# First batch's value loads, masks and weight split rebuilt, seven-product sums kept in PSUM, and a new order of work, in a banded attention and gated MLP kernel

## The chip, the cores and the metric

The kernel runs on one core of one Trainium2 chip. The metric is the device time of one execution in microseconds; three runs of the kernel before are given, and the median counts.

## What is computed

Eight batches, eight heads, 576 positions, head size 64. Four heads ("near") see the last 32 positions, four ("far") see every fourth of the last 128. The attention output is laid out as 576 x 512 per batch and goes through a gated MLP with a spatial product. Cut to what matters:

```python
scores = scale * np.matmul(q, k.transpose(0, 1, 3, 2))
scores = np.where(masks[None], scores, -1e9)          # near heads: mask_plain, far heads: mask_dil
attn = np.exp(scores - scores.max(-1, keepdims=True))
attn = attn / (attn.sum(-1, keepdims=True) + 1e-09)
x = (attn @ v).transpose(0, 2, 1, 3).reshape(B, S, H * D)
h = np.maximum(x @ w_in, 0.0)                          # 512 -> 1024
u, v = h[..., :512], h[..., 512:]
v_n = (v - mean(v)) / np.sqrt(var(v) + 1e-06)
v_s = np.einsum('ts,bsd->btd', w_spatial, v_n) + b_spatial[None, :, None]
out = (u * v_s) @ w_out                                # 512 -> 512
```

`w_in` and `w_out` arrive as 64-bit floats, all else as 32-bit floats.

## The kernel before

Every product that needs full precision is made of three passes over a high and a low part (`PASSES`, L276). The far heads' positions are reordered on the host, so that both kinds of head become a band: 18 blocks of 32 queries against 64 keys each.

**Planner.** The class `Timeline` (L26 to L142) runs at build time. Each piece of work is a generator ("strand") that asks for buffers by tag, waits for keys that other strands have set, and names an engine and a cost per step. The planner takes the strand whose start plus a small weight times its rank is lowest, and so fixes the order on every engine (L1094). Ranks come from the formulas and the tables `shift`, `second` and `first` (L930 to L1028). The tables hold no work, only order. All loads go through SP's queue, in the order of the list `first` (L916). Eight PSUM banks (`bank`) are shared; `mm` (4), `s`, `pt` and `av` limit how many of a kind are open.

**Start.** `warm` (L889) issues 512-column products of zeros whenever TensorE has nothing better, as long as the planner's time is under 30 us. The masks are made on GpSimd and copied into place on VectorE (L229 to L253). `weight` (L300) splits each 512-column half of `w_in` and each quarter of `w_out`, 12 pieces in all, from a 64-bit float into two parts: a scaled copy on ScalarE (L319), a shift with the sign masked out (L321), a merge of the sign (L323), a mask (L326) and a product (L329) on VectorE. The low part is then finished by TensorE (L335 to L339), VectorE or GpSimd. `spatial` (L365) splits the spatial weight; for two of its four large pieces TensorE makes the difference (L381, L382), for the others VectorE does.

**Attention of one batch.** `heads_in` and `values_in` load a head pair. `values_in` (L443) uses four DMAs per pair, each of 64 partitions with pieces of 64 values (256 bytes). `unit` (L455) does a sixth of a batch: products of 64x32 tiles (L469), scaling with the mask added (L489), the row maximum (L491), then for `u < 2` six exponentials with the running sum (L497) and for `u == 2` a subtraction on GpSimd (L504), one exponential (L506) and the sum on VectorE (L508). The result is scaled (L512) and transposed (L517). `weighted` (L526) multiplies by the values (L545) in two halves per group of two head pairs, and `evacuated` (L566) copies each into `raw` (L572).

**MLP of one batch.** `features_in` (L576) splits `raw` into two parts; `v_tile` (L599) makes the second half of `h` and normalises it; `upper` (L681) makes the first half in batch 0; `gate` (L699) makes the spatial product and multiplies (L718). The product with `w_out`, and from batch 1 on the one for `u`, use a seven-product scheme on 2 x 2 blocks. `factor` (L775) splits the factors, `differences` (L812) makes them on GpSimd, `product` (L824, matmul L831) makes one product, and `piece` (L846) adds it in: product 11 is copied by ScalarE (L874), every other product is added to a running tile by VectorE (L872). Per half `m` that is one copy and seven adds; finished tiles go to `out` through SP (L883). There are 15 such sums (8 for `o`, 7 for `u`), each with two halves.

Of the kernel before, what the change touches and what calls it, by code (L numbers as in the profile page):

```python
# [22 lines left out]
NEG = -(2.0**100)  # L23

# [123 lines left out]
def tile_banded_attention_gated_moe(  # L148
# [22 lines left out]
    nc = tc.nc  # L171
# [29 lines left out]
    def bufs(tag, shape, n, pool=const):  # L201
# [6 lines left out]
            mm=[None] * 4,  # L208
            s=[None] * 2,
# [20 lines left out]
    kinds = tl.bufs["raw"][0][:, : 2 * KW].bitcast(BF16).rearrange("p (n k) -> p n k", n=4)  # L230
# [20 lines left out]
    for (far, g), n in cut.items():  # L251
        r = slice(g % 2 * 2 * QB, g % 2 * 2 * QB + 2 * QB)
        nc.vector.tensor_copy(masks[r, US * far + g // 2], kinds[r, n])  # L253
# [4 lines left out]
    nc.vector.tensor_scalar_mul(minus, draft, -1.0)  # L258
    ident = plus.bitcast(F32)
    halfneg = const.tile([P, 1], F32, name="halfneg")  # L260
    nc.gpsimd.memset(halfneg, -0.5)

# [13 lines left out]
    PASSES = ((0, 0), (0, 1), (1, 0))  # L276
    PE, ACT, DVE, DVE2, POOL, DMA = "PE", "ACT", "DVE", "DVE2", "POOL", "DMA"
# [8 lines left out]

    staged = {}

    def weight_in(key, src):

        yield "kqv"
        (staged[key],) = yield DMA, 1.95, 1.5
        dtype = src[0].dtype
        place = staged[key][1][:, : 512 if dtype == F32 else 1024]
        rows = P // len(src)
        for i, part in enumerate(src):
            nc.sync.dma_start(place[i * rows : i * rows + rows].bitcast(dtype), part)
        tl.done("in", *key)

    def weight(key, hi, lo, dtype, how):  # L300
# [23 lines left out]
        tl.add(-0.15 + key[-1] * 0.01, rounded(hi, g, ("hi", *key)))  # L324
# [34 lines left out]
    def spatial_in(sc):  # L359
        yield "kqv"  # L360
        (staged[sc],) = yield DMA, 1.1, 1.5
        nc.sync.dma_start(staged[sc][1][:, :S], w_spT[:, sc, :])
        tl.done("in", sc)

    def spatial(sc):  # L365
# [6 lines left out]
        if sc < 4:  # L372
            nc.scalar.copy(wt[0][:, sc, :], w)
            if not (sc in (1, 2,)):
                yield DVE2, 0.75
                sub(wt[1][:, sc, :], w, wt[0][:, sc, :])
            for ts in (slice(0, HS), slice(HS, S)) if sc in (1, 2,) else ():
# [45 lines left out]
    def heads_in(b, hp, lo=0, hi=NU):  # L423
# [5 lines left out]
        got = yield DMA, 0.74 * (hi - lo), 1.5  # L429
# [13 lines left out]
    def values_in(b, hp):  # L443

        yield "kqv"
        (big,) = yield DMA, 3.3, 1.5
        src = vw[b, hp].rearrange("k (t j d) -> k t j d", j=2, d=D)
        dst = big[1][:, :BIG].rearrange("p (t n d) -> p t n d", n=2, d=D)
        for j in range(2):
            for n in range(2):  # L450
                nc.sync.dma_start(dst[j * D : j * D + D, :, n, :], src[n * QB : n * QB + KW, :, j, :])
# [3 lines left out]
    def unit(b, G, u):  # L455
# [3 lines left out]
        yield [("qk", b, hp, u) for hp in pairs] + ([("v", 0, 1)] if b == 1 else [])  # L459
        yield "s bank bank p"  # L460
        *held, pb = yield PE, 0.52, 0.0
        s = [h[:, : US * KW].rearrange("p (e k) -> p e k", e=US) for _, h in held[1:]]
        for e in range(US):
            for q in range(4):
                g = 2 * (US * u + e) + q // 2
                kq = keys[b, pairs[q % 2]]
                for j in range(2):
                    r = slice(j * D, j * D + D)
                    nc.tensor.matmul(  # L469
                        s[j][q * QB : q * QB + QB, e, :],  # L470
                        kq[r, WIN + S :].rearrange("p (u n i t) -> p u t n i", n=2, i=QB, t=US)[:, u, g // 2 % US, g % 2],
                        kq[r, g * QB : g * QB + KW],
                        start=True,
                        stop=True,
                    )
# [7 lines left out]
        if G >= NG // 2:  # L483
            m = masks[:, US + US * u : 2 * US + US * u]
        else:
            m = masks[:, :US] if u == 0 else masks[:, 1:2].broadcast_to([P, US, KW])
        yield DVE, 1.08, 0.08
        for j in range(2):
            nc.vector.scalar_tensor_tensor(p[:, :, j, :], s[j], SCALE, m, op0=ALU.mult, op1=ALU.add)  # L489
        tl.give(*held)  # L490
        nc.vector.tensor_reduce(nm, flat, axis=AX.X, op=ALU.max, negate=True)  # L491
        if u < 2:
            for e in range(US):
                yield ACT, 0.664 + 0.115 * (e == US - 1), 0.1 * (e == US - 1)
                for j in range(2):
                    i = 2 * e + j
                    nc.scalar.activation(  # L497
                        p[:, e, j], p[:, e, j], AF.Exp, bias=nm[:, i : i + 1], accum_out=sm[:, i : i + 1]
                    )
            nc.scalar.activation(sm, sm, AF.Copy, bias=1e-9)  # L500
            yield DVE, 0.11, 0.085
        else:
            yield POOL, 0.79, 0.04
            nc.gpsimd.tensor_add(flat, flat, nm.unsqueeze(2).broadcast_to([P, 2 * US, KW]))  # L504
            yield ACT, 0.425, 0.1
            nc.scalar.activation(p, p, AF.Exp)  # L506
# [53 lines left out]

    raws = {}

# [118 lines left out]
    def upper(b, h, f):  # L681
        fs = slice(f * P, (f + 1) * P)
        ts = slice(h * HS, h * HS + HS)
        yield [("v", b, t) for t in range(4)] + [("wi", 0, c) for c in range(NC)]
# [475 lines left out]
```

## Time and profile before

| | |
|---|---|
| runs, us | 547.47, 547.51, 550.34 (median 547.51) |
| span of the profiled execution, us | 544.7 |
| around the span (median less span), us | 2.8 |
| PE busy | 536.1 us, 98% |
| DVE / ACT / POOL busy | 80% / 56% / 39% |
| TensorE clock, mean over the span | 1.000 |
| instructions | 18357 |
| moved by DMA | 56.65 MB, of 97446 packets 78290 under 512 B |

The span runs from the first to the last instruction of the core. The profiled execution's own time is not listed apart; its span and the 2.8 us around it make 547.5 us. PE is TensorE, DVE is VectorE, ACT is ScalarE, POOL is GpSimd, SP is the engine that issues the DMAs. A busy time of PE includes the pipelined ends of its products, so it says that something is under way, not that the array is at its peak.

### The profile page before, as it was taken

Reading aid. Unit: us, or ns where it says so; the run is one execution under the profiler, and the core shown is the slowest. Engines: PE = TensorE matmul, PEld = TensorE weight load, DVE = VectorE, ACT = ScalarE, POOL = GpSimd, SP = SyncE. Lnnn points to the kernel's source line nnn. Section 1 sums busy time; section 2 is a strip of 40 time slices with the busy share of each in tenths; the row PEclk is TensorE's granted clock in tenths of the full one; section 3 lists DMA queues with packets and bytes.
Section 4 is the critical chain, followed back from the end, with each engine's and each line's share of the span. In section 5 each row is a group of like instructions: output and inputs, shape, how many; then the busy total and the mean of one; then the engine's idle time right before and its main releaser. Section 6 shows DMA issues by size and latency. Waiting matters only on the chain.

```text
span 544.7 us, 18357 instructions
## 1 busy us (share of the span) xinstructions
PE 536.1 (98%) x7591; PEld 487.9 (90%) x7591; DVE 435.7 (80%) x1036; ACT 307.1 (56%) x939; POOL 215.1 (39%) x255
## 2 busy tenths in 40 slices
PE   9998999999999999999999999999999999999997
PEld 7766789999998899988999999988999899989997
DVE  5988778989956998489957998489956899479836
ACT  4787796455755555565454555556464565454312
POOL 3420385373426153524417163433417153253230
PEclk9999999999999999999999999999999999999999
DMA  8999741201463144511464135421454134301002
GB/s 236 250 185 339 162 105 59 91 22 66 109 160 91 45 134 90 150 52 55 113 127 132 45 113 106 122 75 56 113 121 147 44 113 94 65 12 44 34 1 87
DMA packets 97446, 56.65 MB, mean 104 GB/s; under 512 B 78290, under 2 KB 87506, under 8 KB 97364
## 3 DMA queue, kind: packets, MB, share of 16 engines
q1 hardware_dynamic: 97364, 55.50, 38.4%
q8 instruction: 59, 0.97, 0.8%
q14 instruction: 23, 0.19, 0.1%
HBM read 46.04 MB, written 9.44 MB: 102 GB/s over the span
## 4 chain that ended last, share of the span: by engine, by line
PE 93%; DMA 3%; ACT 2%; issue 1%; SPq 1%; DVE 0%; POOL 0%
PE bank L831 31%; PE bank L711 19%; PE bank L614 16%; PE bank L545 6%; PE bank L469 5%; PE bank L517 3%; PE bank L628 2%; PE bank L690 2%; PE bank L895 2%; PE bank L713 2%; PE bank L712 2%; PE bank L335 1%; DMA kqv<-in_vw_dram 1%; DMA kqv<-in_w_in_dram 1%; ACT p L497 1%
## 5 line engine op out<-in xcount | busy, mean ns | idle before, releaser
L872 DVE TENSOR_TENSOR ur<-ur,bank 128x288 f32<-128x288 f32 x210 | 87.4, 446 | 28.3 <-PE bank L831 27.9
L794 ACT CAST fac<-ur 128x288 fp32r<-128x288 f32 x112 | 46.0, 430 | 79.8 <-DVE ur L718 40.3
L711 PE MATMUL bank<-wth,vnh 128*128 128x288 f32 x256 | 76.5, 299 | 0.0
L280 DVE TENSOR_TENSOR fac<-ur,fac 128x288 fp32r<-128x288 f32 x112 | 60.5, 550 | 19.5 <-ACT fac L794 19.2
L711 PE MATMUL bank<-wth,vnl 128*128 128x288 f32 x256 | 75.6, 295 | 0.1
L711 PE MATMUL bank<-wtl,vnh 128*128 128x288 f32 x256 | 75.6, 295 | 0.0
L821 POOL TENSOR_TENSOR ur<-ur,ur 128x288 f32<-128x288 f32 x64 | 55.5, 877 | 44.1 <-DVE ur L718 34.0
L512 POOL TENSOR_TENSOR p<-p,rv 128x384 f32<-128x384 f32 x48 | 40.8, 851 | 74.5 <-DVE rv L510 63.4
L497 ACT ACTIVATE p<-p,nm 128x64 f32<-128x64 f32 x192 | 64.5, 337 | 8.8 <-DVE nm L491 8.7
L650 POOL TENSOR_TENSOR rs<-rs,halfneg 128x1 f32<-128x1 f32 (+1 forms) x40 | 29.3, 732 | 91.1 <-DVE rs L648 91.0
L831 PE MATMUL bank<-fac,woh 128*128 128x288 f32 x256 | 53.3, 298 | 0.1
L614 PE MATMUL bank<-wih,xl 128*128 128x512 f32 x128 | 50.1, 392 | 1.8 <-issue 1.8
L821 POOL TENSOR_TENSOR raw<-raw,raw 128x288 f32<-128x288 f32 x42 | 43.3, 1037 | 19.4 <-DVE fac L280 18.6
L614 PE MATMUL bank<-wih,xh 128*128 128x512 f32 x128 | 50.4, 394 | 0.0
L614 PE MATMUL bank<-wil,xh 128*128 128x512 f32 x128 | 50.2, 392 | 0.0
L711 PEld LDWEIGHTS bank<-wth,vnh 128*128 128x128 f32 x256 | 48.2, 188 | 0.4
L711 PEld LDWEIGHTS bank<-wth,vnl 128*128 128x128 f32 x256 | 48.1, 188 | 0.3 <-issue 0.3
L711 PEld LDWEIGHTS bank<-wtl,vnh 128*128 128x128 f32 x256 | 48.2, 188 | 0.0
L831 PEld LDWEIGHTS bank<-fac,woh 128*128 128x128 f32 x256 | 42.2, 189 | 2.4 <-ACT raw L572 0.4
L831 PE MATMUL bank<-fac,o 128*128 128x288 f32 x288 | 44.1, 297 | 0.0
L718 DVE SCALAR_TENSOR_TENSOR ur<-ur,bank 128x288 f32<-128x288 f32 x64 | 27.8, 447 | 19.7 <-PE bank L713 19.2
L831 PEld LDWEIGHTS bank<-fac,o 128*128 128x128 f32 x288 | 40.6, 188 | 1.6
(155 smaller groups left out, 1364.5 us busy)
## 6 DMA issues: line engine op xcount, KB each, us to landing
kqv<-in_vw_dram SPq DMA_DIRECT2D x128, 144.0 KB, 3.8
out_dram<-ur SPq DMA_DIRECT2D x64, 144.0 KB, 1.8
kqv<-in_kT_dram SPq DMA_DIRECT2D x30, 304.0 KB, 4.3
kqv<-in_qT_dram SPq DMA_DIRECT2D x30, 288.0 KB, 3.8
kqv<-in_w_in_dram SPq DMA_DIRECT2D x16, 256.0 KB, 5.5
kqv<-in_w_out_dram SPq DMA_DIRECT2D x4, 512.0 KB, 8.4
kqv<-in_w_spT_dram SPq DMA_DIRECT2D x5, 288.0 KB, 6.7
kqv<-in_kT_dram SPq DMA_DIRECT2D x2, 192.0 KB, 5.1
```

What stands on the lines that cost most here:

```text
L280: nc.vector.tensor_sub(out, a, b.bitcast(F32))
L497: nc.scalar.activation(p[:, e, j], p[:, e, j], AF.Exp, bias=nm[:, i : i + 1], accum_out=sm[:, i : i + 1])
L512: nc.gpsimd.tensor_mul(flat, flat, rv.unsqueeze(2).broadcast_to([P, 2 * US, KW]))
L545: nc.tensor.matmul(acc[j][1][1][i * D : i * D + D, (g - h * HB) * QB : (g - h * HB + 1) * QB], v[r, g, :], probs[b, G, u][1][r, e, q * QB ...
L614: nc.tensor.matmul(pm, x[c][a][:, cols], wi[w][:, c, NF:], start=c == 0 and n == 0, stop=c == NC - 1 and n == 2)
L650: nc.gpsimd.tensor_tensor(rs[:m], rs[:m], halfneg[:m], op=ALU.pow)
L711: nc.tensor.matmul(pv, vn[c][a][:, fs], wt[w][:, c, ts], start=n == 0, stop=False)
L718: nc.vector.scalar_tensor_tensor(ur, ur, 0.0, pv, op0=ALU.max, op1=ALU.mult)
L794: nc.scalar.copy(dst[:, 0, i, :], src)
L821: nc.gpsimd.tensor_sub(at(*to), at(*a), at(*c))
L831: nc.tensor.matmul(bank[:, :HS], left(i, w)[:, m * P : m * P + P], right, start=n == 0, stop=n == 5)
L872: op(ob[1], mine[src][1], bank[:, :HS])
```

## The change

The rank tables are replaced (`SHIFT`, `SECOND`, `FIRST`, `RANKS`), and so is the order of the first loads (`LOADS`). What else differs is below; `rows_in` is added but no load of the list uses it. `WAYS` states who finishes each low part: the same as before for `w_in` and `w_out`, and for the spatial weight one piece by TensorE (P) where it was two. `ALONG` states which units use six exponentials with a running sum: one of six in batch 0 (it was four), and the same four as before in the other batches.

```diff
+LOADS = """
+kq1b kq1a kq0a wi00 wi10 bias kq2 kq0b wi12 wi13 kq3 v0 sp4 wi03 v1 wi11 v2 wo1 sp0 wi02 wo2 v3 sp3 sp1 sp2
+wi01 wo3 wo0
+""".split()
+WAYS = {'wi1': 'GPDP', 'wi0': 'PPPP', 'wo': 'PPDP', 'sp': 'DDPD'}
+ALONG = {0: '010000', 1: '110110'}
...
+            ch=[None] * 4,
...
-    for r in range(QB, P, QB):
-        nc.vector.tensor_copy(kinds[r : r + QB], top)
-    nc.vector.tensor_copy(masks, kinds[:, 0:1].broadcast_to([P, US + NS, KW]))
...
+    nc.scalar.activation(work.tile([P, 1], F32, tag="rs", name="first", bufs=4), zeros[:, :1].bitcast(F32), AF.Exp)
...
+    def masks_in():
+        yield DVE, 0.7
...
+        tl.done("masks")
...
-        nc.scalar.activation(g, g, AF.Copy, scale=2.0**-112)
+        nc.scalar.activation(g, g, AF.Prelu, scale=2.0**-112, alpha=-(2.0**32))
         yield DVE2, 0.43
-        nc.vector.tensor_scalar(ti, gi, 3, 0x7FFFFFFF, op0=ALU.logical_shift_left, op1=ALU.bitwise_and)
-        yield DVE2, 0.68
-        nc.vector.scalar_tensor_tensor(gi, gi, 0x80000000, ti, op0=ALU.bitwise_and, op1=ALU.bitwise_or)
...
+        nc.vector.tensor_scalar(gi, gi, 3, None, op0=ALU.logical_shift_left)
...
     def values_in(b, hp):
 
         yield "kqv"
-        (big,) = yield DMA, 3.3, 1.5
...
+        if b == 0:
+            (big,) = yield DMA, 1.6, 1.5
             for n in range(2):
...
+                nc.sync.dma_start(big[1][n * KW : n * KW + KW, :BIG], vw[b, hp, n * QB : n * QB + KW, :])
...
+        if b == 0:
+            for w, e in itertools.product(range(2), range(US)):
+                kind = cut.get((G >= NG // 2, 2 * (US * u + e) + w), 0)
+                nc.tensor.matmul(s[w][:, e, :], spread, kinds[:QB, kind], start=e == 0, stop=True, skip_group_check=e > 0)
...
+        if b == 0:
+            yield DVE, 0.8 if along else 1.4, 0.08
+            tops = nm.rearrange("p (e n) -> p n e", n=2)
+            for w in range(2):
+                nc.vector.tensor_reduce(tops[:, w], s[w], axis=AX.X, op=ALU.max, negate=True)
+            if along:
+                nc.vector.tensor_scalar_mul(nm, nm, SCALE)
+            else:
+                for w in range(2):
+                    nc.vector.tensor_tensor(p[:, :, w], s[w], tops[:, w].unsqueeze(2).broadcast_to([P, US, KW]), op=ALU.add)
+                tl.give(*held)
...
+    def weighted_rows(b, G, rank):
...
+        yield [("pT", b, G, u) for u in range(NU)] + [("values", b, hp) for hp in pairs]
+        yield "av bank av bank av bank av bank raw raw"
+        got = yield PE, 2.1, 0.0
...
+    def evacuated_rows(b, hp, n, far, acc):
+        src, dst = acc[1][1][:, :HS], raws[b, hp][1]
+        if far:
+            yield ACT, 0.36 + 0.36 + 0.25, 0.1
...
-    def product(bank, b, kind, m, left, name):
+    def product(bank, b, kind, m, left, name, fresh):
...
-                bank[:, :HS], left(i, w)[:, m * P : m * P + P], right, start=n == 0, stop=n == 5
+                bank[:, :HS], left(i, w)[:, m * P : m * P + P], right, start=fresh and n == 0, stop=n == 5, skip_group_check=not fresh
...
+    def piece(b, kind, m, name, left):
...
+        before = {"2": "11", "3": "2", "4": "3", "22": "1"}.get(name)
+        which = b, kind, m, name == "22"
+        if before:
+            yield [made(before)]
+        else:
+            yield "mm bank" if name == "21" else "ch bank"
         held = yield PE, 0.8
+        held = open_banks.pop(which) if before else held
...
+        of = {"21": "11", "1": "3", "22": "2"}.get(name)
+        if of:
+            yield [made(of)]
+            yield DVE, 0.372, 0.08
+            ob = mine[of]
+            nc.vector.tensor_add(ob[1], ob[1], bank[:, :HS])
+        else:
+            yield "ur"
+            (ob,) = yield ACT, 0.3, 0.1
+            mine[name] = ob
+            nc.scalar.copy(ob[1], bank[:, :HS])
```

So in the new `piece` products 2, 3 and 4 go on adding in the bank of product 11, and product 22 in that of product 1. Each of the four waits until the bank's earlier state has been read out. Per half `m` there are four copies on ScalarE and three adds on VectorE. `weighted_rows` is used in batch 0 alone: it holds four banks at once for a whole group of two head pairs, and `evacuated_rows` makes three copies in place of one for each far result. Of the first loads, the order by name: `kq` keys and queries of a pair, `wi` and `wo` weights, `v` values, `sp` spatial weight.

## Rows read from the trace of the kernel before

**Rows 1.** The page's part 1: busy time, share of span, instructions.

```profile
PE 536.1 (98%) x7591; PEld 487.9 (90%) x7591; DVE 435.7 (80%) x1036; ACT 307.1 (56%) x939; POOL 215.1 (39%) x255
```

**Rows 2.** Two stretches: length, busy of PE, PEld, DVE, ACT, POOL, clock, DMA, GB/s.

```profile
100.00:150.00 50.00, 50.00 (x589) 46.06 (x588) 47.31 (x117) 26.46 (x87) 25.69 (x29) 1.00 0.21 55
530.00:545.00 15.00, 11.37 (x84) 10.88 (x82) 9.81 (x25) 3.88 (x10) 2.32 (x3) 0.97 0.22 79
```

**Rows 3.** Groups of instructions by line, the whole span: the filling products.

```profile
L895 PE MATMUL bank<-vnl 128*128 128x512 f32 x91 | 25.1, 424 | 1.0 <-DVE vnl L225 1.0
```

**Rows 4.** Timeline of PE: start, length, line, count, idle before.

```profile
34.46 2.30 PE L545 MATMUL bank<-pT,kqv 64*64 64x32 f32 x144
...
44.30 0.90 PE L545 MATMUL bank<-pT,kqv 64*64 64x32 f32 x48
...
51.19 0.40 PE L614 MATMUL bank<-wih,xl 128*128 128x512 f32 x1 [1.83 <-issue]
```

**Rows 5.** Stretches of the start, columns as in rows 2.

```profile
5.00:29.00 24.00, 23.74 (x373) 18.15 (x372) 20.71 (x51) 18.05 (x63) 7.37 (x8) 1.00 1.05 261
29.40:40.20 10.80, 10.27 (x176) 7.00 (x174) 9.31 (x20) 8.87 (x23) 2.62 (x3) 1.00 0.95 187
40.20:55.00 14.80, 12.97 (x187) 9.49 (x187) 12.12 (x24) 11.54 (x22) 0.00 (x0) 1.00 1.01 333
```

**Rows 6.** Timeline of SP's queue: the value loads of batch 0.

```profile
22.47 3.50 SPq L451 DMA_DIRECT2D kqv<-in_vw_dram  x4
...
29.40 10.69 SPq L451 DMA_DIRECT2D kqv<-in_vw_dram  x8
```

**Rows 7.** One tensor's instructions, 0 to 48 us: the values' DMAs until landing.

```profile
DMA to landing us min/median/max: 3.3/6.1/8.2
```

**Rows 8.** Groups by line, 0 to 60 us: VectorE and ScalarE in the start.

```profile
L323 DVE SCALAR_TENSOR_TENSOR kqv<-kqv,mid 128x512 uint32<-128x512 uint32 x12 | 9.4, 781 | 0.5
L319 ACT ACTIVATE kqv<-kqv 128x512 f32<-128x512 f32 x12 | 8.2, 686 | 0.1
L497 ACT ACTIVATE p<-p,nm 128x64 f32<-128x64 f32 x24 | 8.0, 337 | 2.3 <-DVE nm L491 2.3
...
L497 ACT ACTIVATION_READ_ACCUMULATOR p<-p,nm 128x1 f32 x24 | 4.5, 188 | 0.0
...
L572 ACT COPY raw<-bank 128x288 f32<-128x288 f32 x8 | 3.7, 573 | 1.2 <-PE bank L545 1.2
...
L489 DVE SCALAR_TENSOR_TENSOR p<-bank,masks 128x192 f32<-128x192 f32 x12 | 3.6, 340 | 0.6 <-PE bank L469 0.6
L491 DVE TENSOR_REDUCE nm<-p 128x6 f32<-128x384 f32 x6 | 3.3, 553 | 0.2
...
L319 ACT ACT_TABLE_LOAD x1 | 1.3, 1283 | 7.7 <-DMA kqv<-in_w_in_dram 7.7
...
L506 ACT ACTIVATE p<-p 128x384 f32<-128x384 f32 x2 | 1.1, 530 | 0.0
```

**Rows 9.** The chain of waits in the start: start, length, what.

```profile
51.59 0.49 PE bank L381 x2
```

**Rows 10.** Groups by line, the whole span: the two ways of reading a product.

```profile
L872 DVE TENSOR_TENSOR ur<-ur,bank 128x288 f32<-128x288 f32 x210 | 87.4, 446 | 28.3 <-PE bank L831 27.9
...
L874 ACT COPY ur<-bank 128x288 f32<-128x288 f32 x30 | 11.9, 397 | 10.5 <-PE bank L831 9.8
```

**Rows 11.** The chain of waits in a middle batch, columns as in rows 9.

```profile
302.42 1.20 PE bank L469 x72
303.62 1.00 PE bank L831 x6
...
327.33 0.80 PE bank L831 x6
```

**Rows 12.** The end of the chain of waits, columns as in rows 9.

```profile
532.19 9.29 PE bank L831 x68
...
541.51 0.45 DVE ur L872
```

More of the change, by code (lines that the diff above doesn't have):

```diff
@@ new lines @@
+FIRST = {
+    ('differences', 0): 0.43,
+    ('differences', 1): 0.09,
+    ('differences', 2): 0.05,
+    ('factor', 0): -0.1,
+    ('factor', 10): 0.13,
+    ('factor', 2): -0.27,
+    ('factor', 3): -0.16,
+    ('factor', 4): -0.36,
+    ('factor', 7): -0.35,
+    ('factor', 8): -0.92,
+    ('factor', 9): -0.22,
+    ('features_in', 0): -0.45,
+    ('features_in', 1): 0.53,
+    ('features_in', 2): 0.26,
+    ('gate', 0): -0.07,
+    ('gate', 4): 0.03,
+    ('gate', 6): -0.01,
+    ('heads_in', 0): 0.22,
+    ('heads_in', 1): 0.52,
+    ('heads_in', 2): 0.38,
+    ('piece', 11): -0.19,
+    ('piece', 12): -0.33,
+    ('piece', 13): -0.02,
+    ('piece', 14): 0.49,
+    ('piece', 15): -0.04,
+    ('piece', 16): 0.13,
+    ('piece', 17): 0.08,
+    ('piece', 18): 0.27,
+    ('piece', 19): -0.1,
+    ('piece', 2): 0.03,
+    ('piece', 20): -0.17,
+    ('piece', 21): 0.74,
+    ('piece', 22): -0.12,
+    ('piece', 23): 0.15,
+    ('piece', 24): -0.34,
+    ('piece', 25): -0.1,
+    ('piece', 26): 0.91,
+    ('piece', 27): 0.14,
+    ('piece', 3): -0.14,
+    ('piece', 5): 0.1,
+    ('piece', 6): 0.58,
+    ('piece', 9): 0.06,
+    ('unit', 0): 0.41,
+    ('unit', 1): -0.27,
+    ('upper', 0): -0.39,
+    ('upper', 1): -0.14,
+    ('upper', 2): -0.03,
+    ('upper', 5): -0.81,
+    ('upper', 7): -0.06,
+    ('v_tile', 0): -0.25,
+    ('v_tile', 1): -0.15,
+    ('values_in', 1): 0.34,
+    ('values_in', 2): 0.62,
+    ('values_in', 3): 0.27,
+    ('weighted', 0): 0.21,
+    ('weighted', 1): 0.16,
+    ('weighted_rows', 0): 0.1,
+    ('weighted_rows', 1): -0.34,
+    ('whole', 0): -0.03,
+    ('whole', 1): 0.3,
+    ('whole', 6): 0.15,
+}
@@ L784, in factor @@
             yield [("fac", b - 1, "o", n) for n in ("11", "21", "1", "2", "3", "22", "4")]
+        order = [n for n in ("11", "21", "1", "2", "3", "22", "4") if kind == "o" or len(n) == 1]
+        if name != order[0]:
+            yield [("begun", b, kind, order[order.index(name) - 1])]
         yield "fac"
@@ L857, in piece @@
             yield [("prod", b, kind, chain[chain.index(name) - 1] if name in chain else "1", m)]
-        yield "mm bank"
+        before = {"2": "11", "3": "2", "4": "3", "22": "1"}.get(name)
+        which = b, kind, m, name == "22"
+        if before:
+            yield [made(before)]
+        else:
+            yield "mm bank" if name == "21" else "ch bank"
         held = yield PE, 0.8
+        held = open_banks.pop(which) if before else held
         bank = held[1][1]
-        product(bank, b, kind, m, left, name)
+        product(bank, b, kind, m, left, name, before is None)
@@ L889, in warm @@
+        r, h = {"21": (0, 0), "1": (1, 1), "22": (0, 1), "4": (1, 0)}.get(name, (None, None))
+        if r is None:
+            return
+        if kind == "u":
+            raw[b, h, 2 * r + m] = ob
+            tl.done("u", b, h, 2 * r + m)
+            return
+        now = tl.now
+        nc.sync.dma_start(out[b, (2 * r + m) * P : (2 * r + m) * P + P, h * HS : h * HS + HS], ob[1])
+        tl.now += 2.5
+        tl.give(ob)
+        tl.now = now
     def warm():
@@ L923, in tile_banded_attention_gated_moe @@
-    for n, strand in enumerate(first):
-        tl.add(2 * n - 200, strand)
+            key = "wi", half, c
+            loads[f"wi{half}{c}"] = weight_in(key, src)
+            loads[f"w{c}"] = rows_in(c, tuple(w_in[h * D : h * D + D] for h in heads))
+            tl.add(RANKS[key], weight(key, wi[0][:, c, cols], wi[1][:, c, cols], w_in.dtype, who[WAYS[f"wi{half}"][c]]))
     for c in range(NC):
-        tl.add((-1.16, -0.95, -0.74, -0.38)[c], weight(("wo", c), wo[0][:, c, :], wo[1][:, c, :], w_out.dtype, ways[2][c]))
+        key = "wo", c
@@ L1021, in tile_banded_attention_gated_moe @@
-    first = {
-        ("features_in", 2): 0.15,
-        ("upper", 2): 0.03,
-        ("upper", 5): -0.15,
-        ("whole", 0): -0.03,
-        ("whole", 1): 0.3,
-        ("whole", 6): 0.15,
-    }
+        loads[f"sp{c}"] = spatial_in(c)
+        tl.add(RANKS["sp", c], spatial(c))
+    tl.add(RANKS[("masks",)], masks_in())
+    loads["bias"] = bias_in()
+    tl.add(RANKS[("bias",)], bias())
+    for hp in range(NPAIR):
+        loads[f"kq{hp}"] = heads_in(0, hp)
+        loads[f"kq{hp}a"] = heads_in(0, hp, 0, 1)
+        loads[f"kq{hp}b"] = heads_in(0, hp, 1, NU)
+        loads[f"v{hp}"] = values_in(0, hp)
@@ L1029, in tile_banded_attention_gated_moe @@
+    for n, name in enumerate(LOADS):
+        tl.add(2 * n - 200, loads[name])
     turns = {}
@@ L1034, in put @@
         key = strand.__name__, turn
-        rank += shift.get(key, 0.0) + second.get(key, 0.0) * (b == 1) if b else first.get(key, 0.0)
+        rank += SHIFT.get(key, 0.0) + SECOND.get(key, 0.0) * (b == 1) if b else FIRST.get(key, 0.0)
         tl.add(rank, strand)
```

543 lines of the change are left out of this document (348 added, 195 removed).

## The prediction

> **What bounds the kernel now.** I first read the page's busy shares [rows 1]. TensorE is busy 98% of the span, and the stretch table [rows 2] shows why this matters: from 100 to 150 us it has work without a gap, at the full clock. VectorE is at 95% of that stretch, but TensorE doesn't wait for it. Relief of VectorE in the middle of the kernel is worth nothing unless TensorE's own order gets shorter.
>
> So I looked for time in which TensorE is busy and gains nothing. The groups by line show 91 filling products of zeros, 25.1 us of busy time [rows 3]. All lie in the start, where the planner has nothing else to issue. The timeline [rows 4] shows what the start waits for: the first attention products with the values (L545) begin at 34.46 us, the second group at 44.30 us, and at 51.19 TensorE stands for 1.83 us with no releaser shown.
>
> What sets these dates is in the stretches of the start [rows 5]. The DMA engines are fully used (1.05, 0.95, 1.01) up to 55 us, while the rate falls to 187 GB/s between 29.4 and 40.2 us and is 333 GB/s afterwards. SP's queue [rows 6] names the cause: these 10.8 us are the eight value DMAs of the second group, and four more end their issue at 25.97. With up to 8.2 us to land [rows 7] the latter arrive at about 34.2 us, when L545 starts. VectorE is at 86% in each of the two first stretches [rows 5], ScalarE at 75% and 82%: DMA is first, VectorE close behind.
>
> At the end, the last 68 products take 9.29 us, then one add and the store follow [rows 12].
>
> **The change part by part.**
>
> *Values in whole rows.* 16 DMAs of 144 KB become 8 of twice the size, in rows of 4.6 KB in place of 256-byte pieces. The bytes stay, 2.36 MB. At 187 GB/s they take 12.6 us, at 333 GB/s 7.1 us [rows 5]: a saving of 5.5 us. The low end is nothing (the rate stays), the high end takes SP's queue, where twelve issues took 14.2 us [rows 6], so sixteen about 19: half as many save 9.5 us. I take 5.5. SP is in order, so what is queued behind the values gains the same: the last weights and batch 1's keys. In the new list both near value loads also stand ahead of less: 512 KB less before the second, 1.5 us at 333 GB/s.
>
> *VectorE in the start.* The sign merge L323 goes, 12 x 0.781 = -9.4 us. Units: before, 12 x 0.340 + 6 x 0.553 for scaling and maximum, and two sums of the same shape as the maximum, 1.1 us, = 8.5 us [rows 8]. After: twelve half-size maxima, 0.28 (half of L491) to 0.34 each, ten adds at 0.34, five sums at 0.553 = 9.5 to 10.2 us, so +1.0 to +1.7. The spatial piece that TensorE leaves is one subtraction of 576 columns, about 0.8 by scaling L323's 512. Net about -7 us. The mask copies only move later, past the start of batch 0.
>
> *ScalarE in the start.* 24 exponentials and 24 sum reads (8.0 + 4.5 us) become six of each (3.1 us); two whole exponentials become five (+1.6): -7.8 us [rows 8]. Each of the four far results is copied in three pieces instead of one of 0.573: eight more instructions, between 0.2 and 0.4 us by L497's two rows, +1.6 to +3.2. One spatial piece less: two copies of 288 columns, -0.8. Net -5.4 to -7. The table load of 1.28 us, which now follows the first weight's landing, goes ahead of it. Prelu I take at L319's 0.686; below stands the case that it isn't so.
>
> *TensorE.* The spatial piece: two pairs at 0.49 us or a little more [rows 9], -1.2 us with the closing products. The mask products are 36 of 64 columns. Between a 64-column product's 17 ns (1.20 us by 72, [rows 11]) and a filling product's 0.28 us [rows 3] they cost 0.6 to 10 us. I take the low end, being nearest in size, plus a change of tile shape per unit, 0.2 us by the group of six that takes 1.00 right behind 64x32 tiles and 0.80 elsewhere [rows 11]: 2 us. All of it falls where filling products stand now, so it costs nothing; without that cover, 2 us. The whole-group `weighted_rows` waits for three units where a half waited for two, but 144 products already start together at 34.46 [rows 4]: nothing.
>
> *Sums in open banks.* VectorE loses 4 of 7 adds: 15 x 2 x 4 = 120 x 0.446 = -53.5 us; ScalarE gains 90 copies x 0.397 = +35.7 us [rows 10], on 307 us of busy time. As TensorE already runs without gaps, that is worth nothing directly. The new waits are 15 x 2 x 4 = 120: products 2, 3, 4 and 22 each wait for a read of their own bank. Behind the waiting product stands all of TensorE's queue. The cover is the other half's product, six passes in 0.80 us [rows 11], against a read of 0.40 to 0.45 us plus two signals and the product's pipelined end, 0.30 us: it just fits for 2 to 3 and 1 to 22; the other two have more between them. I take nothing, with up to 0.2 us for each of the 60 tight ones (12 us) as the bad end.
>
> *The end* keeps its shape: the last product's add becomes a copy, 0.446 against 0.397.
>
> *New order of work.* The sum that decides is that of the start: DMA -5.5, VectorE -7, ScalarE about -6. The smallest governs, so TensorE's real work moves some 5.5 us ahead into the filling time, and TensorE's own work falls by 1.2. Together -6.7 us, against the profiled execution's 544.7 + 2.8 = 547.5, which is the median too. I round to **541.0 us** (-6.5, 1.2%).
>
> **The rivals.**
>
> *Another bound holds the start.* For it: VectorE's 86% and the chain of weight splits, each step of which waits for the one before; a shorter DMA time helps only if the split follows. Against: both its engines lose 6 to 7 us as well. Then about 2 us are gained: 545.5.
>
> *The middle shortens too.* The new tables order every batch. Each run of small-tile products costs about 0.2 us at its edge [rows 11], and lower load on VectorE lets units be placed in fewer runs. Three runs less in seven batches give 4 us, with the start 537.
>
> *TensorE waits for the reads.* This ends slower. Place: products 3 and 22, 60 in all. It decides when ScalarE's or VectorE's queue holds the read back: at 0.11 us each the gain of 6.5 is used up, at 0.16 the kernel is over 0.5% slower, at 0.2 it takes 541 + 12 = 553. For it: VectorE's 95% at 100 to 150 us, ScalarE in order with casts of 0.4 us. Against: VectorE falls by 53 us, and before no add kept TensorE waiting.
>
> *The leaky rectifier is not in the exponential's table.* In the trace Copy, Exp and Relu share one load of 1.283 us [rows 8]; Prelu doesn't occur. If it needs another table, each of six units can force two changes among the 12 splits: up to 12 x 1.283 = 15.4 us on ScalarE in the start. Its free time there takes half, so +7.7: 548.7. [...]
>
> **How the numbers follow.** Chances: forecast 0.60, other bound 0.14, middle too 0.11, waits for reads 0.10, table changes 0.05. About 0.5% (2.7 us) is what a measurement of this kernel can tell from no change: faster is below 544.8, slower above 550.2. The forecast gives nearly all its 0.60 to faster; the shorter middle 0.11; of the other bound 0.03 is faster and 0.11 same. The waits split 0.03 same, 0.07 slower; the tables 0.02 and 0.03. That makes faster 0.74, same 0.16, slower 0.10. The range starts at 535: the shorter middle gives 537, the DMA's high end 4 us less than the forecast, 537 too, and a part of both may come together. It ends at 547.5, which takes in the other bound and, at its edge, the low end of the DMA saving; it leaves out the waits and the tables.
>
> **What would show it.** Right: fewer than 70 filling products of L895's kind, the first value products before 30 us and the second group before 39, no stretch of the start near 187 GB/s, TensorE without a gap from 100 to 150 us as before, VectorE's busy time lower by about 60 us, ScalarE's higher by some 29. The other bound: value loads early but L545 still after 33 us. The waits: TensorE idle in front of the gathering products, released by ScalarE or VectorE, with busy time missing from 100 to 150 us [rows 2]. The tables: more than one table load. The forecast is wrong if the start is shorter by 5 us and the span isn't.

## The result, and the profile after

The kernel after takes 554.06 us (median; 553.2 to 556.83) against 548.39 for the kernel before, timed beside it: ratio 1.0108, 95% interval 1.007 to 1.0147. Forecast were 541.0 us, a range of 535 to 547.5, and faster with a chance of 0.74. So the sign was wrong and the time lies outside the range. The span rose by 6.4 us, from 544.7 to 551.1.

Where the 6.4 us lie is read from one repeated mark. In the chain of waits, eight 512-column products (line 628 of the kernel before, line 1012 of the kernel after) stand together once per batch. In the kernel before one such group starts at 171.06 us and the one five batches on at 481.48; in the kernel after they start at 178.57 and 486.58. Cut at these two marks, the table of stretches (columns as in [rows 2]) gives start, middle and end. Before:

```profile
0.00:171.06 171.06, 166.98 (x2534) 143.88 (x2535) 140.92 (x328) 112.97 (x341) 73.37 (x90) 1.00 0.58 149
171.06:481.48 310.42, 309.22 (x4651) 287.23 (x4651) 248.26 (x600) 173.36 (x550) 124.67 (x145) 1.00 0.35 93
481.48:544.70 63.22, 59.89 (x408) 56.81 (x407) 46.51 (x111) 20.72 (x48) 17.02 (x20) 1.00 0.11 38
```

After:

```profile
0.00:178.57 178.57, 166.06 (x2549) 142.69 (x2550) 134.16 (x313) 111.16 (x326) 72.06 (x88) 0.96 0.55 143
178.57:486.58 308.01, 308.00 (x4652) 287.67 (x4651) 216.73 (x521) 190.06 (x610) 121.63 (x145) 1.00 0.34 93
486.58:551.10 64.52, 60.37 (x409) 56.98 (x407) 37.75 (x85) 25.95 (x64) 16.27 (x20) 1.00 0.11 38
```

The start is 7.5 us longer, the middle 2.4 shorter, the end 1.3 longer. In the start TensorE is busy for 0.9 us less, but stands for 12.5 us (178.57 less 166.06) where it stood for 4.1. And its mean clock there is 0.96. From 100 to 150 us nothing is lost: the first row of [rows 2] has this answer after:

```profile
100.00:150.00 50.00, 49.96 (x588) 46.25 (x587) 47.92 (x102) 29.99 (x89) 25.90 (x27) 1.00 0.13 41
```

The page's part 1 [rows 1] and its clock row show the same from afar: TensorE from 98 to 97%, VectorE 47 us lower, ScalarE 20 us higher, and a granted clock of 0.7 to 0.9 in three of the first five slices.

```profile
PE 534.4 (97%) x7606; PEld 487.3 (88%) x7606; DVE 388.6 (71%) x917; ACT 327.2 (59%) x1000; POOL 210.0 (38%) x253
...
PEclk9897899999999999999999999999999999999999
```

What TensorE waits for stands in the list of its waits (total, times, longest):

```profile
PE bank L628 <- issue: 3.6, 1, 3.6
PE bank L907 <- DMA kqv<-in_vw_dram: 2.8, 3, 1.0
PE bank L772 <- DMA kqv<-in_qT_dram: 2.1, 1, 2.1
PE bank L907 <- issue: 1.3, 1, 1.3
```

Of these, 4.9 us are waits for loads (2.8 and 2.1), and another 4.9 (3.6 and 1.3) have no releaser that the profile shows. L907 is the old L545 in batch 0: the products that need the values; L772 gathers from keys and queries. The chain of waits shows how the value loads hold them (start, length, what):

```profile
22.36 9.30 DMA kqv<-in_vw_dram
...
31.70 1.35 PE bank L907 x72
...
33.05 1.25 issue
...
35.20 11.67 DMA kqv<-in_vw_dram
...
46.92 3.19 PE bank L907 x145
...
54.82 1.22 PE bank L628
```

These two value loads take 9.3 and 11.7 us. The view of that tensor, the answer to [rows 7], has all eight:

```profile
DMA to landing us min/median/max: 8.4/9.2/11.7
```

The median was 6.1 before, but for DMAs of half the size, so the two don't compare. The stretches of [rows 5] do: the one at 187 GB/s is at 237 now, the faster one behind it fell from 333 to 279, and the first from 261 to 248.

```profile
5.00:29.00 24.00, 21.15 (x365) 15.91 (x367) 16.82 (x51) 11.46 (x30) 5.72 (x6) 0.93 1.03 248
29.40:40.20 10.80, 8.08 (x168) 5.71 (x165) 7.30 (x18) 6.04 (x14) 1.66 (x2) 1.00 1.04 237
40.20:55.00 14.80, 8.95 (x177) 6.15 (x177) 11.14 (x22) 8.79 (x18) 1.22 (x1) 0.79 1.03 279
```

The last rows that answer to rows of before, from the groups by line: fillers [rows 3], the two ways of reading a product [rows 10], the scaled copy and the table load [rows 8].

```profile
L1293 PE MATMUL bank<-vnl 128*128 128x512 f32 x60 | 18.8, 455 | 1.0 <-DVE vnl L495 1.0
...
L1263 DVE TENSOR_TENSOR ur<-ur,bank 128x288 f32<-128x288 f32 x90 | 39.4, 446 | 29.0 <-PE bank L1219 28.0 <-ACT ur L1268 0.4
L1268 ACT COPY ur<-bank 128x288 f32<-128x288 f32 x120 | 47.2, 398 | 62.8 <-PE bank L1219 62.3
...
L614 ACT ACTIVATE kqv<-kqv 128x512 f32<-128x512 f32 x12 | 8.1, 672 | 9.6 <-DMA kqv<-in_w_in_dram 9.2 <-DMA kqv<-in_w_out_dram 0.3
...
L528 ACT ACT_TABLE_LOAD x1 | 1.3, 1283 | 0.7 <-PEq L1445 0.7
```

### The profile page after: what moved, and what is told of

It reads as the page before. It is cut to its first block, busy times and chain, and to the rows that moved or that the text cites. A ratio compares the mean times of both kernels' runs of the same rounds, so it can differ in the third digit from the quotient of the medians.

```text
span 551.1 us, 18317 instructions
## 1 busy us (share of the span) xinstructions
PE 534.4 (97%) x7606; PEld 487.3 (88%) x7606; DVE 388.6 (71%) x917; ACT 327.2 (59%) x1000; POOL 210.0 (38%) x253
## 4 chain that ended last, share of the span: by engine, by line
PE 89%; DMA 6%; issue 1%; SPq 1%; POOL 1%; DVE 0%; ACT 0%; POOLq 0%
PE bank L1219 31%; PE bank L1095 18%; PE bank L998 16%; PE bank L870 6%; PE bank L772 5%; DMA kqv<-in_vw_dram 4%; PE bank L842 3%; PE bank L1012 3%; PE bank L1074 2%; PE bank L1097 2%; PE bank L1096 1%; DMA kqv<-in_kT_dram 1%; DMA kqv<-in_w_in_dram 1%; PE bank L628 1%; PE bank L907 1%
## 5 line engine op out<-in xcount | busy, mean ns | idle before, releaser
L1268 ACT COPY ur<-bank 128x288 f32<-128x288 f32 x120 | 47.2, 398 | 62.8 <-PE bank L1219 62.3
L548 DVE TENSOR_TENSOR fac<-ur,fac 128x288 fp32r<-128x288 f32 x112 | 57.3, 517 | 34.2 <-ACT fac L1182 29.1
L1209 POOL TENSOR_TENSOR ur<-ur,ur 128x288 f32<-128x288 f32 x64 | 53.5, 843 | 67.7 <-DVE ur L1102 58.8
L837 POOL TENSOR_TENSOR p<-p,rv 128x384 f32<-128x384 f32 x48 | 41.7, 872 | 83.6 <-DVE rv L835 68.6
L1182 ACT CAST fac<-ur 128x288 fp32r<-128x288 f32 x112 | 47.3, 432 | 41.4 <-DVE ur L1102 28.6
L1263 DVE TENSOR_TENSOR ur<-ur,bank 128x288 f32<-128x288 f32 x90 | 39.4, 446 | 29.0 <-PE bank L1219 28.0
L814 ACT ACTIVATE p<-p,nm 128x64 f32<-128x64 f32 x168 | 56.2, 336 | 4.2 <-DVE nm L808 4.2
L1219 PE MATMUL bank<-fac,woh 128*128 128x288 f32 x256 | 53.8, 300 | 0.0
L998 PE MATMUL bank<-wih,xh 128*128 128x512 f32 x128 | 50.8, 397 | 0.0
L998 PE MATMUL bank<-wil,xh 128*128 128x512 f32 x128 | 50.5, 394 | 0.0
L998 PE MATMUL bank<-wih,xl 128*128 128x512 f32 x128 | 50.4, 394 | 0.0
L1209 POOL TENSOR_TENSOR raw<-raw,raw 128x288 f32<-128x288 f32 x42 | 40.2, 967 | 24.1 <-DVE fac L548 18.2
L1219 PEld LDWEIGHTS bank<-fac,woh 128*128 128x128 f32 x256 | 42.3, 189 | 3.0 <-ACT ur L1268 0.7
L1219 PE MATMUL bank<-fac,o 128*128 128x288 f32 x288 | 43.1, 296 | 1.1 <-ACT fac L1182 0.7
```

Of the source, the lines that this page charges most:

```text
L548: nc.vector.tensor_sub(out, a, b.bitcast(F32))
L814: nc.scalar.activation(p[:, e, j], p[:, e, j] if b else s[j][:, e], AF.Exp, bias=nm[:, i : i + 1], scale=1.0 if b else SCALE, accum_out=sm ...
L837: nc.gpsimd.tensor_mul(flat, flat, rv.unsqueeze(2).broadcast_to([P, 2 * US, KW]))
L998: nc.tensor.matmul(pm, x[c][a][:, cols], wi[w][:, c, NF:], start=c == 0 and n == 0, stop=c == NC - 1 and n == 2)
L1182: nc.scalar.copy(dst[:, 0, i, :], src)
L1209: nc.gpsimd.tensor_sub(at(*to), at(*a), at(*c))
```

## The experiments

The reading after the result, which the runs were to test: whole rows made the value loads no faster. The new plan counts on fast loads, so TensorE, whose order is fixed, stands in front of loads that come late. The value loads and the halves of `w_in` have one thing in common that the keys, queries, `w_out` and spatial pieces don't have: each of their DMAs goes into 64 partitions, and the stretch at 333 GB/s in [rows 5], from which the forecast took its rate, is one in which keys and queries load, into 128. Each kernel was timed beside the kernel before; ratios are to that.

### The layout of the loads: e1, e2, e3, e9, e10

**e1_v128** stacks batch 0's values to 128 rows ahead of the launch and loads a pair with one DMA. The order of the work is that of after, as in the other four of this group.

```diff
-            for n in range(2):
-                nc.sync.dma_start(big[1][n * KW : n * KW + KW, :BIG], vw[b, hp, n * QB : n * QB + KW, :])
+            nc.sync.dma_start(big[1][:, :BIG], vr[hp])
```

> The changed kernel with the first batch's values laid out as 128 rows, one DMA of 128 partitions per pair in place of two of 64. Order on the four compute engines as in the changed kernel. Theory L (loads land later than the plan has them, because a load into 64 partitions moves at some 240 GB/s whatever its rows): value loads land in clearly less than 9.2 us, the stretch 15 to 45 us moves more than 240 GB/s, time 550 to 552. Rival R (the new order of work in the start is worse by itself, whenever loads land): 554, no change.

Measured: 548.88 us, ratio 1.0018 (0.9991 to 1.0045): 5 us below after and a little below the range of L, but no faster than before. TensorE still waits 2.8 us for values.

**e2_vw128** does the same to `w_in` as well; the rows of `w_in` are reordered ahead of the launch so that a chunk of 128 is one piece. The planner's cost of such a load stays as it was, so its order does too.

```diff
-            src = tuple(w_in[h * D : h * D + D, half] for h in heads)
+            src = (w_in[c * P : c * P + P, half],)
```

> As e1_v128, and the eight halves of w_in too as one DMA of 128 partitions each. Order on the compute engines as in the changed kernel. Theory L: rate of the start near 350 GB/s, the waits of TensorE on DMA (2.8 and 2.1 us) and the fall of its clock go, time 542 to 546, under the kernel before. Rival R: 554.

Measured: **540.81 us, ratio 0.9878 (0.9824 to 0.9931)**, faster than both kernels and a little below the range of L, with the compute engines' work in the order of after.

**e3_pieces** is the kernel after with the values in 256-byte pieces again, four DMAs per pair into 64 partitions.

```diff
-                nc.sync.dma_start(big[1][n * KW : n * KW + KW, :BIG], vw[b, hp, n * QB : n * QB + KW, :])
+                for j in range(2):
+                    nc.sync.dma_start(dst[n * KW : n * KW + KW, :, j, :], src[n * QB : n * QB + KW, :, j, :])
```

> The changed kernel with the first batch's values in 256-byte pieces, four DMAs of 64 partitions per pair, as the kernel before has them, into the new layout. Theory L: the whole rows gave little, so 554 to 558. Rival P (piece size was the price, 5.5 us of DMA time as predicted): 559 to 564.

Measured: 553.4 us, ratio 1.0112 (1.0053 to 1.0171), the time of after, 0.6 us below the range of L. Undoing the whole rows costs nothing, so they had bought nothing. The 16 value DMAs, again of the old size, land in a median of 6.3 us, as before the change (6.1).

**e9_w128** changes `w_in` alone (the diff of e2 on the kernel after).

> The kernel after, with the weights' halves (w_in) alone in DMAs of 128 partitions (rows of w_in put in the order of the partitions before the launch, so that each chunk is one piece of memory); the values stay in two DMAs of 64 partitions, the order of the work is that of after. Theory P (a load into 64 partitions moves some 240 GB/s, into 128 up to 400): 16 of the start's 24 loads of 64 partitions go, so most of the late dates go with them: between the run with the values alone (548.9) and that with both (540.8), about 544 to 548, 15 to 45 us at 260 to 300 GB/s, but the eight value DMAs still land in 8 to 9 us and TensorE still waits for them. Rival T (there is one threshold: the plan works only when everything is on time): 550 to 554. Rival W (the weights are the whole cause, the values follow): 540.5 to 542.5, no wait for values.

Measured: 548.88 us, ratio 1.0022 (0.9994 to 1.005), a little above the range of P and below that of T. The rate came out inside P's, but the wait that P named did not: only 0.2 us for the values, and 7.6 us of "issue" in its place.

```profile
PE bank L907 <- issue: 4.4, 1, 4.4
PE bank L628 <- issue: 2.3, 1, 2.3
...
PE bank L772 <- issue: 0.9, 1, 0.9
...
PE bank L907 <- DMA kqv<-in_vw_dram: 0.2, 1, 0.2
```

The loads of one kind alone give 5.2 us each, both together 13.2, so the parts don't add. Why isn't shown: what is left is a wait for values in e1, and time with no releaser in e9.

**e10_halves** separates partitions from the number of DMAs: e2 with each of its 12 loads cut in two again, by columns, so that both halves go into 128 partitions.

```diff
-            nc.sync.dma_start(big[1][:, :BIG], vr[hp])
+            for n in range(2):
+                cols = slice(n * BIG // 2, (n + 1) * BIG // 2)
+                nc.sync.dma_start(big[1][:, cols], vr[hp, :, cols])
```

> The kernel with values and w_in in 128 partitions (540.8), where each of these 12 loads is again two DMAs, but by halves of the columns: both go into 128 partitions. Number and size of the DMAs are then those of after (24, 256 and 288 KB), and the rows are half as long (2 KB and 2.3 KB); the order of the work is the same. Theory P (the number of partitions sets the rate): 540 to 542.5, 15 to 45 us at 300 GB/s or more. Rival N (the number of DMAs or their size sets it, the partitions don't matter): 549 to 555, 15 to 45 us near 240 GB/s.

Measured: 543.01 us, ratio 0.9901 (0.987 to 0.9932), half a microsecond above the range of P and 6 below that of N. With as many DMAs of the same sizes as after, 11 us of after's time are gone. What no run separates from the partitions is the order of the rows in the chip's memory: e1, e2, e9 and e10 all read a copy laid out anew.

One row of each kernel's stretches decides this group: 15 to 45 us, the last columns being clock, DMA share and GB/s. After:

```profile
15.00:45.00 30.00, 24.80 (x476) 18.33 (x476) 22.86 (x57) 18.36 (x46) 7.70 (x7) 0.94 1.03 238
```

e3, with 256-byte pieces:

```profile
15.00:45.00 30.00, 26.59 (x479) 19.68 (x481) 22.34 (x55) 17.55 (x45) 7.72 (x7) 0.89 1.09 240
```

e1, with the values in 128 partitions:

```profile
15.00:45.00 30.00, 25.54 (x423) 18.77 (x420) 20.66 (x53) 16.78 (x43) 7.20 (x7) 0.83 1.03 282
```

e9, with `w_in` in 128:

```profile
15.00:45.00 30.00, 23.49 (x441) 17.10 (x432) 21.08 (x51) 15.91 (x41) 7.19 (x7) 0.89 0.99 269
```

e10, with both, in twice as many DMAs:

```profile
15.00:45.00 30.00, 26.29 (x580) 19.34 (x579) 27.94 (x65) 20.83 (x52) 6.94 (x7) 0.96 0.97 355
```

e2, with both, and below it e2's fastest 10 us:

```profile
15.00:45.00 30.00, 26.47 (x611) 19.56 (x601) 27.40 (x65) 20.65 (x52) 7.61 (x7) 1.00 0.86 319
...
15.00:25.00 10.00, 10.00 (x245) 7.94 (x238) 9.75 (x26) 6.37 (x22) 4.69 (x4) 1.00 1.03 412
```

The DMA share is about 1.03 at 238 GB/s and at 412 alike. So a full share says here that the DMA engines are occupied, not how much they move. (e2's 0.86 is a mean over the 30 us: from 35 to 45 us its share is 0.67.)

The three stretches of e2, cut at its marks at 166.99 and 474.80, show where after loses time:

```profile
0.00:166.99 166.99, 161.63 (x2549) 139.91 (x2550) 134.78 (x313) 110.78 (x326) 72.84 (x88) 1.00 0.49 153
166.99:474.80 307.81, 307.81 (x4651) 287.57 (x4651) 216.54 (x521) 190.23 (x610) 121.78 (x145) 1.00 0.34 93
474.80:539.50 64.70, 60.37 (x408) 56.99 (x407) 37.46 (x85) 25.88 (x64) 16.29 (x20) 0.99 0.11 38
```

Its start has the same 2549 products as after's and is 11.6 us shorter. Of these, 7.2 us are idle time (12.5 less 5.4) and 4.4 us are busy time: the same products, slower. After's stretches show the clock (third column from the end) at 0.50 in two places:

```profile
18.00:21.00 3.00, 3.00 (x52) 2.54 (x53) 2.17 (x9) 2.12 (x12) 1.67 (x2) 0.50 1.09 262
...
47.00:48.50 1.50, 1.50 (x99) 1.50 (x100) 0.00 (x0) 0.89 (x2) 0.00 (x0) 1.00 1.09 230
49.00:51.00 2.00, 2.00 (x36) 1.26 (x32) 1.94 (x3) 1.47 (x4) 0.00 (x0) 0.50 1.02 247
51.00:54.50 3.50, 0.26 (x1) 0.00 (x0) 3.08 (x6) 0.92 (x4) 0.00 (x0) 0.50 1.02 369
55.00:58.50 3.50, 3.50 (x8) 2.40 (x9) 0.00 (x0) 1.57 (x6) 0.00 (x0) 0.50 1.04 407
```

The first follows a wait of 2.14 us for queries that ends at 16.81. The second follows waits of 0.80 and 0.98 us for values, the last of which ends at 46.92: the clock fell between 48.5 and 49, ahead of the long stand without a releaser (51.26 to 54.82), and was full again at 59. From 55 to 58.5 TensorE is busy throughout. e2 keeps 1.00 over its whole start. The four rows at 0.50 hold 8.76 us of busy time. In after's timeline products of 512 columns (L998) begin every 0.43 us from 56.69 to 58.40, at a clock of 0.50, and every 0.23 us from 59.13 to 61.63, at 1.00. At 1.00 the work of the four rows would so take some 4.1 us less, an estimate from these rows and dates, and that is nearly the whole difference in busy time.

### Telling the plan the truth: e4, e6

**e4_costs** keeps the loads of after and gives the planner costs worked out from about 240 GB/s; the tables stay, the order of the work follows from both.

```diff
-    ISSUE, HALF, BOTH = 0.3, 2.1, 3.0
+    ISSUE, HALF, BOTH = 0.3, 2.2, 3.0
...
-            (big,) = yield DMA, 1.6, 1.5
+            (big,) = yield DMA, 2.4, 1.5
```

> The changed kernel, its planner alone told load costs as the trace shows them (all at about 240 GB/s). Theory L: TensorE's order now has filling products or other work where it waited, time 546 to 550. Rival R: 554 or more, since the tables of ranks stay.

Measured: 552.32 us, ratio 1.0072 (1.0044 to 1.01), between the ranges of L and R. It is 1.7 us below after, and the intervals overlap. The waits for loads are gone from TensorE's list but for 0.2 us, and it issues 84 fillers where after has 60, at the same 240 GB/s: a plan that knows the rate can't make the loads come earlier.

**e6_costs128** is e2 planned anew with costs from some 400 GB/s (1.35, 1.5 and so on in the same places), under the same tables.

> e2_vw128 with its planner told that all first loads move at about 400 GB/s, as they do there (values 1.5, w_in and w_out 1.35 per 512 KB, spatial weight 0.75, keys and queries 0.5 per third). Theory D: the order uses the earlier landings, 536 to 540. Rival: the tables of ranks were made for other dates, and a new order under them is no better or worse, 541 to 546.

Measured: 600.1 us, ratio 1.0949 (1.0902 to 1.0996), a miss for both. The loads don't hold it (the DMA share is 0.75 from 15 to 45 us); in the list of waits TensorE stands longest for GpSimd's scaling of the attention rows (L837) and for split factors (L1182).

```profile
PE bank L842 <- POOL p L837: 28.4, 4, 9.2
PE bank L1219 <- ACT fac L1182: 7.6, 4, 2.9
```

Fed with better dates these rank tables gave an order 59 us worse. Whether tables sought anew would do better wasn't tried.

### The layout under the old order: e5, e11

**e5_before_w128** is the kernel before with `w_in` in 128 partitions, **e11_before_vw128** with the values as well; the order of the work is that of before.

> The kernel before with one edit: each half of w_in comes as one DMA of 128 partitions in place of two of 64 (its rows reordered on the host). Order of work on the compute engines as before. Theory D (loads land earlier, but TensorE's fixed order can use that only where it waited): the weights land earlier, the rate of the start rises above 300 GB/s, time 544.5 to 547. Rival W (the shape of the loads alone makes the gain of e2, whatever the plan): 540 to 542.

> The kernel before, in its own order of work, with the weights' halves and the first batch's values in DMAs of 128 partitions (both laid out as 128 rows before the launch): the layout that took the kernel after from 554 to 540.8, without any part of the change but the number of the values' DMAs. Theory S (the layout only lets a plan's dates be met; what is gained under them is the plan's and the edits'): the old order has late dates of its own and no use for early values, so 543 to 546, near the 545.6 with the weights alone, and the middle stays at 62 us a batch. Rival Y (the layout is the whole gain of the fast kernel and the change adds nothing): 540 to 542, value products before 31 us.

Measured: e5 545.57 us, ratio 0.9966 (0.9944 to 0.9989), inside the range of D, though the rate from 15 to 45 us is 260 GB/s and not above 300; e11 544.27 us, ratio 0.9946 (0.9929 to 0.9963), inside that of S. In e11 the last value load is issued at 24.4 us, where it was 39.5 before, but the chain of waits has the first value products where they were in [rows 4], at 34.5 us:

```profile
34.54 1.25 PE bank L548 x72
```

The old order fixes them there. The layout alone is worth 0.5%, and layout, edits and new plan together 1.2% (e2), with intervals that just touch.

### Undoing one part of the fast version: e7, e8

**e7_adds** is e2 with one copy and seven adds per sum, each product in a bank of its own, as before; **e8_merge** is e2 with the sign merge on VectorE in place of the leaky rectifier. Both were planned anew under the same tables.

```diff
-            nc.scalar.activation(g, g, AF.Prelu, scale=2.0**-112, alpha=-(2.0**32))
+            nc.scalar.activation(g, g, AF.Copy, scale=2.0**-112)
...
+            nc.vector.scalar_tensor_tensor(gi, gi, 0x80000000, ti, op0=ALU.bitwise_and, op1=ALU.bitwise_or)
```

> e2_vw128 with the seven products added on VectorE as in the kernel before (one copy, seven adds per half; every product in a bank of its own), planned anew under the same tables. Theory G (the open banks shorten the middle): a batch takes about 62.0 us again in place of 61.5, time 543 to 546. Rival T (the new tables shorten it): a batch stays at 61.5 to 61.6, time 540 to 541.5.

> e2_vw128 with the weight split of the kernel before: a scaled copy on ScalarE and the sign merge on VectorE, 12 more instructions of about 0.78 us there, planned anew under the same tables. Theory S (VectorE bounds the start once loads come early): 543 to 547. Rival: VectorE has room, 540 to 541.5.

Measured: e7 547.45 us, ratio 1.0 (0.9973 to 1.0027), and e8 546.88 us, ratio 0.9991 (0.9962 to 1.0019). e7 is 1.4 us above the range of G, e8 just inside that of S, and each loses 6 to 7 us against e2. From 100 to 150 us TensorE is no longer full. First e7, then e8:

```profile
100.00:150.00 50.00, 48.60 (x531) 44.13 (x530) 47.87 (x119) 27.13 (x89) 20.66 (x26) 1.00 0.17 49
```

```profile
100.00:150.00 50.00, 48.03 (x571) 43.80 (x570) 45.77 (x106) 32.05 (x109) 24.47 (x28) 1.00 0.19 54
```

Neither number is the price of its part. e6 shows what a new plan under these tables can do by itself, and the merge belongs to the weight split of the start, so what TensorE lacks from 100 to 150 us in e8 probably comes through the order. e7 loses its time between its marks at 110.17 and 235.83 us: 125.7 us, against 118.8 between e2's at 109.65 and 228.48. What the open banks are worth alone stays open. One thing is seen: the four batches behind that, to the mark at 481.69, take 61.5 us each in e7 without open banks (e2: 61.6), so the shorter middle doesn't need them.

## Why the prediction was wrong

**Values in whole rows, -5.5 us: the step that failed.** It read 187 and 333 GB/s from [rows 5] as the rates of short pieces and of long rows. Neither is. The 187 is a mean of two stretches, and a wait of SP's queue lies behind the second (the last line, from the list of SP's waits):

```profile
29.40:37.00 7.60, 7.60 (x166) 5.66 (x165) 6.29 (x14) 5.67 (x16) 1.66 (x2) 1.00 1.13 217
37.00:40.00 3.00, 2.47 (x11) 1.27 (x10) 2.83 (x7) 3.00 (x9) 0.95 (x1) 1.00 0.48 103
...
SPq L451 <- DVE wil L329: 2.8, 1, 2.8
```

While the DMA engines were full the rate was 217 GB/s; then they ran half empty, as SP waited 2.8 us for VectorE to release a buffer before it could issue a value load. The 0.95 of [rows 5] hid that. And the 333 are mostly loads into 128 partitions (5056 of the 5568 KB issued in that stretch: keys, queries, `w_out` and spatial weight), where the values go into 64. Several things differed between the two stretches, and the forecast picked one without a row that holds the others still. e3 undoes the rows and keeps the time, e10 keeps number and size of the DMAs and takes 11 us off. So the term is about nothing in after, where 15 to 45 us run at 238 GB/s. The low end ("the rate stays") was named, but as the end of a range below which nothing was looked for.

Of the partitions the runs show this: from 15 to 45 us after moves 238 GB/s and e10 355, with DMAs of the same number and sizes for values and `w_in`, into 64 partitions in the one and into 128 in the other. Both stretches hold other loads too, and e10 reads copies laid out anew. Of the piece size they show 240 GB/s with 256-byte pieces (e3) against 238 in whole rows (after).

**"What sets these dates", and the new order.** The forecast saw the values land at about 34.2 us, L545 start at 34.46, and took the one for the cause of the other. But in the kernel before TensorE's list of waits names no load, and e11, which has issued the values of the first group at 15.97 us and not at 25.97, starts these products at 34.54: the old order set the date. The plan carries its own rates (1.6 us per pair of values), and TensorE's order is fixed by it. With the rate unmoved, loads that the new plan dates earlier became waits, 4.9 us of them. Early dates on late loads were not among the rivals listed, though they follow from the forecast's own low end: if the rate stays, a plan made for a higher one isn't worth nothing, it costs. The bad end of this term reached down to zero gain only, and that is why the range didn't hold the time.

**TensorE idle, then slow.** Of the 11.6 us that separate after's start from e2's, 4.4 are the same products done more slowly, some 4.1 of them, by the estimate above, in stretches at a clock of 0.50 that come after waits. The forecast had no term for it. Of the 7.2 us of idle time, by the lists of waits some 4.3 are for loads (4.9 less e2's 0.6), and some 2.4 have no releaser (4.9 less 2.5).

**What the forecast's signs showed.** Fewer than 70 fillers: 60, as said, and yet the kernel is slower: what left the filling came back as waiting. The first value products before 30 us and the second group before 39: no. Ten products of the first group start at 30.27 and the rest waits until 31.70; the second starts at 44.43 and waits until 46.92. In e2 they start at 26.37 and 39.00: with the loads on time the signs come. No stretch near 187 GB/s: true, at no gain. A count of fillers needs the idle time beside it.

**VectorE and ScalarE.** VectorE fell by 47 us, not 60: the group of adds lost 48.0 us (87.4 less 39.4) rather than 53.5, and smaller groups grew. In the start it fell by 6.8 (140.92 less 134.16), about the 7 of the forecast. ScalarE rose by 20, not 29. Neither decides anything, as the forecast had it.

**Mask products, 2 us under cover.** Six take 0.28 us in e2's chain, 1.7 us for all 36, and the cover held.

**The rivals.** Another bound of the start: not tested in after, whose value loads weren't early; in e2, where they are, the first value products start at 26.37, not after 33, so its sign isn't there. The wait for reads of open banks fell: in the list of TensorE's waits no product waits for a read, and the weight loads of L1219 wait 0.7 us in all behind ScalarE's copies (L1268). The table changes fell: one load of 1.283 us, with the rectifier at 672 ns a piece. The middle was shorter by 2.4 us of the 4 given; that fewer runs of small tiles did it isn't shown. The end, "keeps its shape", is 1.3 us longer in after and 1.5 in e2; its cause wasn't looked for.

**And the size.** With the loads in 128 partitions the change makes 540.8 us, where the forecast had 541.0. This is luck: the term that gives it is another one, and e2 is another kernel. Its start is 4.1 us shorter than before, where the forecast had 6.7, its middle is 2.6 shorter and its end 1.5 longer. Against e11, the old order with the same layout, it is some 3.5 us faster.

## What to carry to other kernels

A rate read from one stretch belongs to everything that differs in that stretch: before a load is rebuilt for a better rate, cut the stretch finer, to see whether the queue ran dry in it, list the destination's partitions beside the piece size, and find two rows that differ in one only. Try transfers that each span all 128 partitions, even where the data's natural halves want two of 64: here, with the rows laid out anew, 15 to 45 us ran at 355 GB/s (e10) against 238 (after), and the kernel took 543.01 us against 554.06. And when a fixed order is planned on costs, a load that misses its date can cost more than the same load did under the old order (4.9 us of waits for loads in after's list, none in that of the kernel before): first measure the rate, then plan on it. The ranks may then need a new search.

## What was not expected of the hardware

**The share of DMA time doesn't tell the rate:** 1.03 at 238 GB/s (after) and at 412 GB/s (e2).

**"issue" in front of TensorE comes with instruction packets.** The trace has a DMA queue of instruction packets of 16 KB; 59 of them in after's span (0.97 MB in all), one for some 258 of TensorE's 15212 products and weight loads, which is why they are taken for TensorE's here. In the stands named here, which have no releaser, TensorE goes on 2 to 3 us after such a packet began. For after's longest stand, which ends at 54.82 us, the view of the DMA from 52.0 to 52.5 shows it:

```profile
q1 hardware_dynamic: 57, 0.19, 94.9%
q8 instruction: 1, 0.02, 13.1%
```

The same holds for after's 1.25 us (packet between 31.4 and 31.5, TensorE on at 34.30), for the 1.83 us of [rows 4] (between 48.7 and 48.8, on at 51.19), for e9's 2.32 (between 49.0 and 49.5, on at 51.67) and e10's 2.71 (between 40.5 and 41.0, on at 43.31). But other packets of the kind pass without a stand, also where the queues are full. In the kernel before one begins between 29.5 and 29.6 us, with the DMA share at 1.15 from 29.4 to 32.0, and no "issue" stands in front of TensorE until the 1.83 us of [rows 4]. In e11 one begins between 23.0 and 23.5, with the queue of the loads at 90% to 107% in each half microsecond from there to 26.0, and e11 has no "issue" in its list of waits of the first 60 us. So that the packets are the cause is argued from dates alone; no run changed them, and it stays open.

**The clock can fall after a wait and stay down while TensorE is busy.** In after it was at 0.50 from 18 to 21 us, behind a wait of 2.14 us and with TensorE busy for all of it, and from 49 to 58.5, behind waits of 0.80 and 0.98 us and with 3.56 us of standing in it. The same 2549 products took 4.4 us more busy time than in e2. Not every stand has this: behind the 1.83 us of [rows 4] the clock stayed at 1.00, as the last row of [rows 5] shows.
